# Half of a weight-gradient product placed one step earlier, and the first group's transposes in another order

## The chip, the cores and the metric

The kernel runs on one core of one Trainium2 chip. The metric is device time in microseconds (us), the median of several runs; lower is better. Five engines work side by side, each through its own list of instructions: TensorE (PE; its weight loads are PEld), VectorE (DVE), ScalarE (ACT), GpSimd (POOL) and SyncE (SP). The last two, and ScalarE near the end, also issue DMAs. The matrix products leave TensorE through PSUM, from where ScalarE or VectorE copies them out.

## The reference: what is computed

One layer's forward pass and its gradients, for x of 2048 x 576, a hidden width of 4608, and bf16 inputs:

```
g = sigmoid((x * gate_w).sum(-1))
a = irfft2(rfft2(x) * (w_r + 1j * w_i))                # spectral branch
b = (gelu(B_x @ w_gate) * (B_x @ w_up)) @ w_down       # FFN branch
out = g * a + (1 - g) * b
```

The outputs are out and the gradients for x, w_r, w_i, w_gate, w_up, w_down and gate_w. The function takes B_x as a constant, and the kernel reads one x. With dO the gradient of out, and A = gelu(x w_gate) * (x w_up), the FFN's part needs these products: z = dO w_down^T; xy = x [w_gate, w_up]; d_w_down = A^T dB, where dB is dO scaled by 1 - g; d_w_gate and d_w_up = x^T dH, where dH holds the two gradients of the hidden layer; and b and the gradient of x, which sum over the whole hidden width and come in a second phase.

## The kernel before

**Groups and steps.** The hidden width is cut into 18 groups of 256 columns, numbered from 0 (`for g in range(NG)`, L986). A group has four steps (`for m in range(NPR)`, L988); each takes 512 of the 2048 rows as four tiles of 128. In the prediction "third step" is m = 2 and "fourth step" is m = 3 (the sets x1, do1 and do2 of the first group are counted from 1, and its steps are called by m). One step does this:

- `H_mm` (L403) issues z: 16 matmuls of 256 columns (L413) and 4 of half height (L418), into a tile of the PSUM pool `pz`, and then the start of xy (L422). `full` adds 8 matmuls of 512 columns (L429) for each half of xy.
- ScalarE evicts z with the factor 1 - g (`H_da`, da, L441) and each half of xy (`H_act`: q L448, xb L450, hu L451). The tile q of the first half needs a buffer that VectorE's previous step must have left (L489).
- VectorE makes dH and A of it (`H_ew1` L456 to L460, then `H_ew2` L483 to L491, with sigmoids on ScalarE between, s and sg, L476 to L480). SP stores them in DRAM for the second phase (L495).

**Weight gradients one group late.** While group g goes through its steps, TensorE also forms the weight gradients of group g - 1. `W_units` (L514) lists them: w[0] to w[3] are the four row blocks of the d_w product (L553), 16 matmuls of 512 columns each, cut into four pieces of 4 matmuls; d[0] to d[3] are the parts of d_w_down (L535), 16 matmuls of 288 columns each; `tail` (L563) is the last 64 rows of d_w, put between z and xy of the third step. The returned list says which pieces go into which step: entries 0 to 3 are the steps, entry 4 is carried into the first step of the next group (`carry`), and the dictionary holds what is put inside a step. The results go into the pool `pw` (two PSUM banks, tag wps); ScalarE copies each out (L504) and POOL's queue stores it.

**Units of the spectral branch.** From the second group on, the list `fft` (L927) is worked off between the pieces: forward transforms (L596, L613), the middle (L705, L794), and the inverse (L841, L853, L867 with L869). Each unit is 2 to 8 short matmuls into a `pf` tile, and ScalarE copies it out (Y L601 or L603, ve L616, Xx and Xg L710, Vt L797, ZT L844, ZU L856, ev L873). `pf` and `z` are one tag in `pz`, which has a single buffer of two banks. So a unit can't start before the unit or z ahead of it has been copied out. `want` (L951) says how many units a step gets, and the loop at L1081 spreads them over the step's pieces by weight. In the middle part VectorE also forms the spectral products (`side`, L997): L722 to L764, run after `H_ew1` of each step.

**The first group** has no weight gradients to do yet. Its steps transpose x and dO on TensorE instead (`titems`, L370): a set of tiles is three items of 8, 8 and 4 transposes (L378, L384), each into a tile of the pool `pg`, which has two buffers, and a copy on ScalarE (AC) or VectorE (VC) after each (L385). The gate (`gate`, L389; its activation g_bf is L396) takes a `pg` tile too. In step m, x1 is the set of x for step m + 1, and do2 the set of dO for step m + 2. In the code, `early` runs before the first half of xy, `mid_` after it, and `rest` between z's full matmuls and its half-height ones in the next step.

**Order of the work.** Each engine runs its instructions in the order in which the code issues them; nothing moves them later. Semaphores between the engines come from the tile framework. DMAs also share eight semaphores in turn (one can wait for an earlier one that has the same semaphore).

**Second phase.** After the groups, SP loads `pin` tiles (L1126) and `wd_all` (L1145), while TensorE works off the last group's weight gradients (L1148 to L1153); their stores are issued by ScalarE. Then 1.2 thousand matmuls each over `wgT`, `wuT` and `wd_all` (L1201) form the gradient of x and b.

Of the kernel before, what the change touches and what calls it, by code (L numbers as in the profile page):

```python
# [255 lines left out]
def kernel(  # L256
# [246 lines left out]
    def wevac(out, in_):  # L503
        wcopy[0](out, in_)  # L504
# [3 lines left out]
    def dwtile(name):  # L508
        if not spare:
            return stage.tile([P, 2, FG], BF16, tag="dw", name=name)  # L510
        spare.append(spare.pop(0))
        return ew.tile([P, 4, FG], BF16, tag=spare[-1], name=name, bufs=2)[:, 0:2, :]

    def W_units(g):  # L514
        fsl = slice(g * FG, (g + 1) * FG)
        kt = kept[g]

        def tl(k, t):
            tile_ = kt[t // 4][min(k, 1)]
            return tile_[:, t % 4, :] if k == 0 else tile_[:, t % 4, k - 1, :]  # L520
        dwd_tiles, wp = {}, {}

        def halves(f, us):
            return [(us, lambda: f(0)), (us, lambda: f(1))]

        def wtile(key):
            if key not in wp:
                wp[key] = pw.tile([P, TPB, FG], F32, tag="wps", name="wps")
            return wp[key]

        def u_dwd(fch, h):
            def f(half):
                wps = wtile(("d", fch, h)).rearrange("p a b -> p (a b)")
                for t in range(8 * half, 8 * half + 8):
                    nc.tensor.matmul(wps[:, :288], lhsT=tl(0, t)[:, fch * P:(fch + 1) * P],  # L535
                                     rhs=dB[:, t, h * 288:(h + 1) * 288], start=(t == 0), stop=(t == T - 1))
                if half == 0:
                    return
                if h == 0:
                    dwd_tiles[fch] = stage.tile([P, D], BF16, tag="dwd", name="dwd")  # L540
                dwd = dwd_tiles[fch]
                wevac(dwd[:, h * 288:(h + 1) * 288], wps[:, :288])
                if h == 1:
                    r0 = g * FG + fch * P
                    wst[0].dma_start(out_6[r0:r0 + P, :], dwd[:])
            return halves(f, 1.0)

        def u_dw(c, cuts=(0, 4, 8, 12, T)):

            def f(t0, t1):  # L550
                wps = wtile(("w", c))
                for t in range(t0, t1):
                    nc.tensor.matmul(wps[:].rearrange("p a b -> p (a b)"), lhsT=xn[:, t, c * P:(c + 1) * P],  # L553
                                     rhs=kt[t // 4][1][:, t % 4].rearrange("p k f -> p (k f)"), start=(t == 0), stop=(t == T - 1))
                if t1 < T:
                    return
                dw = dwtile("dw")
                wevac(dw[:], wps[:])
                for k, ov in enumerate((o4v, o5v)):
                    wst[0].dma_start(ov[:, c, fsl], dw[:, k, :])  # L560
            return [(3.45 * (b - a) / T, lambda a=a, b=b: f(a, b)) for a, b in zip(cuts, cuts[1:])]

        def tail():  # L563
            wps = wtile("t")
            for t in range(T):
                for k, r in ((1, LO), (2, HI)):
                    nc.tensor.matmul(wps[r, 0, :], lhsT=xn[:, t, 512:576], rhs=tl(k, t),  # L567
                                     start=(t == 0), stop=(t == T - 1))
            dw = dwtile("dwt")
            wevac(dw[:, 0], wps[:, 0, :])  # L570
            wst[0].dma_start(out_4[512:576, fsl], dw[LO, 0, :])
            wst[0].dma_start(out_5[512:576, fsl], dw[HI, 0, :])
        w = [u_dw(c, (0, 12, T)) if g == 0 and c < 2 else u_dw(c) for c in range(4)]
        d = [u_dwd(fch, h) for fch in range(FCH) for h in range(2)]
        if g == 0:
            return [[w[0][:1], w[1][:1]], [w[2]], [d[0], d[1], d[2], d[3]], [w[3][:3]], w[3][3:], {1: [w[0][1][1], w[1][1][1]], 2: [tail]}]
        return [[d[0]], [d[1], d[2], d[3]], [w[0]], [w[1], w[2]], w[3], {2: [tail]}]


    side = []  # L580
# [311 lines left out]
    for c in range(6):  # L892
        w = gwr[0:1, eo(c)] if c < 4 else gwr[0:1, 512:D]
# [83 lines left out]
    carry, pend, held, rest = [], None, [], []  # L977
# [8 lines left out]
    for g in range(NG):  # L986
# [3 lines left out]
        for m in range(NPR):  # L990
# [15 lines left out]
            if g == 0:  # L1006
                def items(src, dst, t, *cp):
                    return titems(src, dst, 4 * t, (pgtile,) * 3, cp) if t < NPR else [None] * 3
                do1 = items(dB, dOT, 1, VC, VC, VC) if m == 0 else []
                do2 = items(dB, dOT, m + 2, AC, AC, VC)  # L1010
                x1 = items(xn, xT, m + 1, AC if m else VC, VC, VC)
                z, xy_full = H_mm(g, m, ([opening] if m == 0 else []) + rest)
                rest = []
                da = H_da(g, m, z)
                if m == 0:
                    early, mid_, late_ = do1[:2], [do1[2], x1[0]], x1[1:]
                elif m < NPR - 1:
                    early, mid_, late_ = x1[:1], x1[1:], []
                else:
                    early, mid_, late_ = [], [], []  # L1020
                for f in early:
                    f()
                xy = xy_full(0)
                for f in mid_:
                    f()
                if held:
                    held.pop()()
                for part in (1, 0):
                    H_act(0, xy, tiles, part)

                def between():
                    for f in late_:
                        f()
                xy = xy_full(1, between)
                for part in range(2):
                    H_act(1, xy, tiles, part)
                if m == 0:
                    build_R(nc, tb, unit, 4)
                    columns_B(nc, tb, res)
                elif m == 1:  # L1040
                    next(makeB)
                if m < NPR - 1:
                    gate(m + 1)
                else:
                    V.tensor_copy(g32[:], g_bf[:])
                    V.tensor_scalar(gs32[:], g32[:], SD2, None, op0=ALU.mult)
                if m + 2 < NPR:
                    do2[0]()
                    rest = do2[1:]
                state += [*H_ew1(g, tiles, da), da]  # L1050
                held.append(sigs)
            else:
                z, xy_full = H_mm(g, m)
                da = H_da(g, m, z)
                for f in inside:
                    f()
                xy = xy_full(0)
                if held:
                    scale_dB(0, AC)
                    held.pop()()  # L1060
                for part in (1, 0):
                    H_act(0, xy, tiles, part)
                k0 = int(n > 0 and pr > 7 and ready())
                xy = xy_full(1, fft_next if k0 else None)
                for part in range(2):
                    H_act(1, xy, tiles, part)
                state += [*H_ew1(g, tiles, da), da]
                if pr == 5:
                    scale_dB(1, AC)
                    scale_dB(2, VC)  # L1070
                    build_R(nc, tb, unit, 8)
                    build_R(nc, tb, unit, 12)
                elif pr == 6:
                    scale_dB(3, VC)
                    next(makeB)
                side_work(4.4)
                jobs = carry + hs
                total = sum(w for w, _ in jobs)
                at, k = 0.0, k0
                tables = {6: 0}.get(pr)  # L1080
                for i, (w, f) in enumerate(jobs):  # L1081
                    if k < n and (at >= total * k / n - 0.45 or len(jobs) - i <= n - k):
                        fft_next()
                        k += 1
                    if i == tables:
                        run_late(tb)
                        wcopy[0] = VC
                    if pr == NG * NPR - 1 and at == 0.0:
                        sigs()
                    f()  # L1090
                    at += w
                wcopy[0] = AC
                while k < n:
                    fft_next()
                    k += 1
                flush()
                if pr == 6:
                    next(makeB)
                if pr < NG * NPR - 1:
                    sigs()  # L1100
# [250 lines left out]
```

## Time and profile before

| | us |
|---|---|
| median of 3 runs (1407.67 to 1407.96) | 1407.94 |
| the profiled execution: device time | 1407.67 |
| its span, from the first to the last instruction | 1405.8 |
| TensorE busy | 1375.1 |
| VectorE busy | 748.8 |
| ScalarE busy | 712.3 |
| the first group, first z to the second group's first z | 8.3 to 45.3 |
| second phase's first matmul | 977.7 |

How to read the profile: times are us from the start of the span. A line of the timeline gives start, length, engine, line of the code, operation, what it writes and reads, its shape and how many follow each other; in square brackets, how long the engine stood idle before it and whose work ended that. A line of the waits gives the waiting instruction, an arrow, whose work it waited for, and then the sum in us, the count and the longest. Matmul ends are modelled: one takes longer than its distance to the next, so that what counts between two is start to start. A matmul of 512 columns takes 0.216 us so (sixteen in 3.45 us); a few records are missing, which the counts show (x11 for 12).

### The profile page before, as it was taken

Reading aid. Unit: us, or ns where it says so; the run is one execution under the profiler, and the core shown is the slowest. Engines: PE = TensorE matmul, PEld = TensorE weight load, DVE = VectorE, ACT = ScalarE, POOL = GpSimd, SP = SyncE. Lnnn points to the kernel's source line nnn. Section 1 sums busy time; section 2 is a strip of 40 time slices with the busy share of each in tenths; the row PEclk is TensorE's granted clock in tenths of the full one; section 3 lists DMA queues with packets and bytes.
Section 4 is the critical chain, followed back from the end, with each engine's and each line's share of the span. In section 5 each row is a group of like instructions: output and inputs, shape, how many; then the busy total and the mean of one; then the engine's idle time right before and its main releaser. Section 6 shows DMA issues by size and latency. Waiting matters only on the chain.

```text
span 1405.8 us, 25935 instructions
## 1 busy us (share of the span) xinstructions
PE 1375.1 (98%) x10182; PEld 913.9 (65%) x10272; DVE 748.8 (53%) x1408; ACT 712.3 (51%) x1309; POOL 246.0 (18%) x486
## 2 busy tenths in 40 slices
PE   8999999999999999999999999999999999999999
PEld 6556566565556556556566566556777777777777
DVE  7975656555888778885666666560000642212101
ACT  7867767777778777767777776661000000000000
POOL 3001111023353633423101111110000100000000
PEclk9999999999999999999999999999999999999999
DMA  6423434355464555556456464849999997778774
GB/s 217 127 81 109 130 109 129 91 143 157 111 160 134 152 156 156 127 145 164 129 140 174 127 167 132 197 116 281 182 193 186 239 190 169 160 160 166 156 152 90
DMA packets 510646, 214.49 MB, mean 153 GB/s; under 512 B 312538, under 2 KB 503708, under 8 KB 510524
## 3 DMA queue, kind: packets, MB, share of 16 engines
q1 hardware_dynamic: 493402, 187.44, 57.2%
q0 software_dynamic: 14912, 24.24, 6.2%
q8 instruction: 80, 1.31, 0.4%
q10 hardware_dynamic: 2210, 1.15, 0.3%
q14 instruction: 42, 0.34, 0.1%
HBM read 41.05 MB, written 93.84 MB: 96 GB/s over the span
## 4 chain that ended last, share of the span: by engine, by line
PE 55%; ACT 1%; DMA 1%; SPq 1%; DVE 1%; issue 1%; ACTq 0%
PE acc L1201 30%; PE wps L553 7%; PE xy L429 7%; PE wps L535 4%; PE z L413 4%; PE wps L567 1%; DMA wd_all<-in_B_w_down_dram 1%; PE xy L422 1%; SPq L1126 1%; PE z L418 1%; PE pf L867 1%; PE pf L869 1%; ACT ZT L844 0%; PE pf L841 0%; ACT hu L451 0%
## 5 line engine op out<-in xcount | busy, mean ns | idle before, releaser
L1201 PEld LDWEIGHTS <-pin 128*128 128x128 bf16 x3456 | 338.0, 98 | 86.2 <-issue 0.9
L553 PE MATMUL wps<-dH,xn 128*128 128x512 bf16 x1124 | 268.1, 379 | 1.5
L429 PE MATMUL xy<-wgu,xT 128*128 128x512 bf16 x1090 | 257.9, 379 | 8.5 <-issue 7.8
L429 PEld LDWEIGHTS <-xT 128*128 128x128 bf16 x1152 | 106.5, 98 | 133.0 <-issue 24.8
L553 PEld LDWEIGHTS <-xn 128*128 128x128 bf16 x1152 | 111.4, 98 | 118.4 <-issue 0.6
L1218 ACT COPY bo<-acc 128x288 f32<-128x288 f32 x32 | 12.7, 398 | 304.4 <-PE acc L1201 279.8
L535 PE MATMUL wps<-dB,A 128*128 128x288 bf16 x1152 | 154.2, 286 | 1.0 <-DVE dB L984 0.9
L560 POOL DMA_DIRECT2D out_dram<-dw x134 | 72.7, 546 | 443.3 <-ACT dw L504 417.8
L1201 PE MATMUL acc<-wgT,pin 128*128 128x288 bf16 x1152 | 143.9, 286 | 0.3 <-ACT dw L504 0.3
L1201 PE MATMUL acc<-wuT,pin 128*128 128x288 bf16 x1152 | 143.6, 286 | 0.0
L1201 PE MATMUL acc<-wd_all,pin 128*128 128x288 bf16 x1152 | 142.6, 286 | 0.0
L413 PE MATMUL z<-wdT,dOT 128*128 128x256 bf16 x1152 | 137.5, 272 | 3.6 <-ACT Xg L710 1.0
L535 PEld LDWEIGHTS <-A 128*128 128x128 bf16 x1152 | 112.1, 98 | 34.7 <-issue 1.9
L413 PEld LDWEIGHTS <-dOT 128*128 128x128 bf16 x1152 | 112.4, 98 | 26.6 <-issue 6.4
L441 ACT ACTIVATE da<-z,omg 128x256 bf16<-128x256 f32 x288 | 112.1, 472 | 16.0 <-PE z L418 15.9
L450 ACT CAST xb<-xy 128x512 bf16<-128x512 f32 x144 | 85.2, 592 | 48.2 <-PE xy L429 48.2
L1273 DVE SCALAR_TENSOR_TENSOR f32t<-gwf,dlog,b16t 128x576 f32<-128x576 f32 x16 | 13.1, 817 | 173.4 <-DMA b16t<-dxa_scr 173.4
L448 ACT ACTIVATE q<-xy 128x512 bf16<-128x512 f32 x144 | 87.7, 612 | 17.1 <-DVE xb L489 8.7
L483 DVE TENSOR_TENSOR xb<-xb,sg 128x1024 bf16<-128x1024 bf16 x48 | 33.2, 692 | 104.1 <-ACT sg L479 104.1
L451 ACT CAST hu<-xy 128x512 bf16<-128x512 f32 x144 | 87.6, 608 | 0.0
L504 ACT CAST dw<-wps 128x512 bf16<-128x512 f32 x72 | 42.2, 588 | 68.2 <-PE wps L553 57.4
L1232 DVE SCALAR_TENSOR_TENSOR b16t<-b16t,g,f32t 128x576 bf16<-128x576 bf16 x16 | 13.1, 819 | 96.1 <-DMA b16t<-a_scr 95.8
(216 smaller groups left out, 1655.3 us busy)
## 6 DMA issues: line engine op xcount, KB each, us to landing
scr<-dH SPq DMA_DIRECT2D x144, 256.0 KB, 3.4
scr<-A SPq DMA_DIRECT2D x72, 256.0 KB, 2.7
out_dram<-dw POOLq DMA_DIRECT2D x134, 64.0 KB, 2.5
wd_all<-in_B_w_down_dram SPq DMA_DIRECT2D x3, 1728.0 KB, 12.2
out_dram<-dwd POOLq DMA_DIRECT2D x34, 144.0 KB, 2.9
scr_p<-Vt SPq DMA_DIRECT2D x32, 145.0 KB, 2.8
wgu<-in_B_w_gate_dram SPq DMA_DIRECT2D x18, 256.0 KB, 4.1
wgu<-in_B_w_up_dram SPq DMA_DIRECT2D x18, 256.0 KB, 3.4
```

What stands on the lines that cost most here:

```text
L413: nc.tensor.matmul(zo(t), lhsT=dOT[:, ci, t, :], rhs=wdT[:, ci, :], start=(t % 4 < 2 and ci == 0), stop=False)
L429: nc.tensor.matmul(xy[k][:, t % 2, :], lhsT=xT[:, ci, t, :], rhs=wgu[:, ci, :], start=False, stop=(ci == 3))
L441: nc.scalar.activation(da[:, t, :], z[:, t % 2, t // 2, :], ACT.Copy, scale=omg32[:, 4 * m + t:4 * m + t + 1])
L448: nc.scalar.activation(q[:, h, :], xy[:, :, 0:FG], ACT.Square)
L450: nc.scalar.copy(xb[:, h, :], xy[:, :, 0:FG])
L451: nc.scalar.copy(hu[:, h, :], xy[:, :, FG:2 * FG])
L483: V.tensor_tensor(xb[:], xb[:], s[:], op=ALU.mult)
L504: wcopy[0](out, in_)
L535: nc.tensor.matmul(wps[:, :288], lhsT=tl(0, t)[:, fch * P:(fch + 1) * P], rhs=dB[:, t, h * 288:(h + 1) * 288], start=(t == 0), stop=(t == ...
L553: nc.tensor.matmul(wps[:].rearrange("p a b -> p (a b)"), lhsT=xn[:, t, c * P:(c + 1) * P], rhs=kt[t // 4][1][:, t % 4].rearrange("p k f -> ...
L560: wst[0].dma_start(ov[:, c, fsl], dw[:, k, :])
L1201: nc.tensor.matmul(acc[:, :288], lhsT=src[:, r, :], rhs=w_of(r)[:, h * 288:(h + 1) * 288], start=(first and r == 0), stop=(last and r == F ...
```

## The change

In the lists of the groups from the second on, the first two of w[1]'s four pieces (8 of its 16 matmuls of 512 columns) stand in the third step's entry, behind w[0], instead of the fourth's. In the first group's steps 1 and 2, two of the three items of x1 run before the first half of xy instead of one; and in steps 0 and 1, two of the three items of do2 run at the end of the step instead of one, so that a single one is left for the next step's z.

```
@@ W_units @@
         if g == 0:
             return [[w[0][:1], w[1][:1]], [w[2]], [d[0], d[1], d[2], d[3]], [w[3][:3]], w[3][3:], {1: [w[0][1][1], w[1][1][1]], 2: [tail]}]
-        return [[d[0]], [d[1], d[2], d[3]], [w[0]], [w[1], w[2]], w[3], {2: [tail]}]
+        return [[d[0]], [d[1], d[2], d[3]], [w[0], w[1][:2]], [w[1][2:], w[2]], w[3], {2: [tail]}]
@@ first group @@
                 if m == 0:
                     early, mid_, late_ = do1[:2], [do1[2], x1[0]], x1[1:]
                 elif m < NPR - 1:
-                    early, mid_, late_ = x1[:1], x1[1:], []
+                    early, mid_, late_ = x1[:2], x1[2:], []
@@ first group @@
                 if m + 2 < NPR:
                     do2[0]()
-                    rest = do2[1:]
+                    do2[1]()
+                    rest = [do2[2]]
```

More of the change, by code (lines that the diff above doesn't have):

```diff
@@ L576, in W_units @@
             return [[w[0][:1], w[1][:1]], [w[2]], [d[0], d[1], d[2], d[3]], [w[3][:3]], w[3][3:], {1: [w[0][1][1], w[1][1][1]], 2: [tail]}]
-        return [[d[0]], [d[1], d[2], d[3]], [w[0]], [w[1], w[2]], w[3], {2: [tail]}]
+        return [[d[0]], [d[1], d[2], d[3]], [w[0], w[1][:2]], [w[1][2:], w[2]], w[3], {2: [tail]}]
     side = []
@@ L1017 @@
                 elif m < NPR - 1:
-                    early, mid_, late_ = x1[:1], x1[1:], []
+                    early, mid_, late_ = x1[:2], x1[2:], []
                 else:
@@ L1048 @@
                     do2[0]()
-                    rest = do2[1:]
+                    do2[1]()
+                    rest = [do2[2]]
                 state += [*H_ew1(g, tiles, da), da]
```

## The prediction

> **What bounds the kernel now.** The page comes first. TensorE is busy for 98% of the span, its clock row shows 9 in all forty slices, and the chain that ended last is 55% TensorE. Only time in which TensorE waits can be won; no matmul is added or removed.
>
> ```profile
> span 1405.8 us, 25935 instructions
> ...
> PE 1375.1 (98%) x10182; PEld 913.9 (65%) x10272; DVE 748.8 (53%) x1408; ACT 712.3 (51%) x1309; POOL 246.0 (18%) x486
> ...
> PEclk9999999999999999999999999999999999999999
> ```
>
> Second, the waits of TensorE from 99 to 853 us, the stretch in which the spectral branch's units lie between the FFN's matmuls.
>
> ```profile
> PE pf L596 <- ACT ve L616: 1.8, 4, 1.1
> PE pf L705 <- ACT Xx L710: 1.8, 4, 0.8
> PE pf L867 <- ACT ZT L844: 1.4, 2, 1.1
> PE pf L705 <- ACT Xg L710: 1.2, 2, 0.6
> PE z L413 <- ACT Xg L710: 1.0, 2, 0.5
> ```
>
> All of them are one wait: a unit (pf) or the next z needs the single PSUM buffer of the pool pz, and ScalarE hasn't yet copied the unit before out of it. Third, where they lie. I cut the timeline at each step's first z matmul, and took each unit's start less the start of the instruction before it and its own length. So counted, the third steps (m = 2) of groups 2 to 15 hold 11.67 us: 0.45, 0.70, 1.09, 1.83, 1.75, 0.84, 0.68, 1.75, 0, 0, 0, 1.51, 0.40, 0.67. The fourth steps hold 2.13 us: 1.13 in group 8, 0.93 in group 10, 0.08 in group 14. (The waits list shows some 0.17 us less for each, since it starts at the modelled end.) Without units a third step lasts 11.38 us (878.44 to 889.83) and a fourth 12.97 (to 902.80): the third has the least to put between units. Here is that of group 9:
>
> ```profile
> 514.63 0.41 PE L705 MATMUL pf<-Vp,Btab 128*128 128x289 bf16 x2
> 514.88 1.89 PE L553 MATMUL wps<-dH,xn 128*128 128x512 bf16 x8
> 517.39 0.41 PE L705 MATMUL pf<-Vp,Btab 128*128 128x289 bf16 x2 [0.62 <-ACT Xg L710]
> 517.63 1.03 PE L553 MATMUL wps<-dH,xn 128*128 128x512 bf16 x4
> 519.17 1.91 PE L413 MATMUL z<-wdT,dOT 128*128 128x256 bf16 x16 [0.51 <-ACT Xg L710]
> ```
>
> After the last unit (517.39) the two copies of L710 start at 517.83, 0.20 us after the next matmul, and take 1.28; z follows 0.05 later. That is 1.53 us, and four matmuls of L553 cover 0.86 (sixteen take 3.45 in the chain): 0.67 us is lost. The unit before is late because ScalarE must first evict the second half of xy (q, xb, hu).
>
> **The third step gets eight matmuls.** In the changed program's order w[1][:2] lies behind w[0] in 16 third steps (groups 2 to 17), and the gaps between units grow: 4, 4, 4 to 8, 4, 8 where four units lie in a step, 4, 8, 4 to 8, 8, 8 where three do. In the fourth step 8, 8, 8 becomes 4, 8, 4 or 8, and 12, 8, 12 becomes 8, 8, 8. No engine's order of work changes else, but that the eviction of w[0] or w[1] falls between other copies; two batches of loads on POOL's queue (Wt, needed a pair of units later) come behind two dw stores; SP's queue keeps its order.
>
> In group 9 the second unit moves from 514.63 to 515.21 (four matmuls, 0.86, less its own wait of 0.29); the third is due at 517.18, ScalarE is free for it at 517.39 as before: 0.21 left. z has 1.73 to cover 1.53. So 1.75 becomes 0.21, and the fourth step (slacks of 2.07, 0.70 and 1.57 us before its units and the next z) keeps none: 1.54 won. The same sum for each group:
>
> Groups 2 to 5. What waits behind q, xb and hu gets 0.86 us more cover; a unit with gap 4 and an idle ScalarE loses only 0.03 to 0.14. Third steps: 0.45, 0.70, 1.09, 1.83 become 0.03, 0.14, 0.41, 1.35 (group 5 keeps its table transposes); fourth steps get 0.03, 0.03, 0.14, 0. **Won 1.9.**
>
> Groups 6 to 11. Here VectorE takes part: q has one buffer, so the step's first q eviction waits until VectorE has finished the step before.
>
> ```profile
> ACT q L448 <- DVE xb L489: 8.4, 5, 2.6
> ```
>
> This is from ScalarE's waits between 330 and 640 us. It strikes fourth steps: q starts there 6.4, 6.7, 7.3, 7.9 and 8.2 us after z in groups 6, 7, 8, 10, 11, against 5.5 in others. VectorE runs through there without a gap, so its times stand while the fourth step now starts later: q comes 0.2 to 1.7 us earlier in the step, at 6.2, 5.8, 6.1, 6.2, 6.5. Third steps: 1.75, 0.84, 0.68, 1.75, 0, 0 become 0.20, 0, 0.12, 0.21, 0, 0; fourth: group 8 1.13 to about 1.4 (the dw copy now precedes the unit's copy), group 10 0.93 to 0.66. But a shorter fourth step leaves VectorE late in the next group. After group 6 its first copy (L483) waits for nothing in three steps on end, so the unit at 398.94 can't come earlier: all 1.55 is lost again. After group 7 (0.84) some 0.5 stays, after group 10 nothing, while group 9's is kept (VectorE idles 1.55 us in the next step). Passed on: 0, 0.5, 0.25, 1.54, 0, 0. **Won 2.3.**
>
> Groups 12 to 17. Third steps 13 to 15: 1.51, 0.40, 0.67 to 0.84, 0, 0.04 (ZT takes 1.02 us, and stays late once in group 13). Group 14's fourth step has five units and now gaps of 4, 4, 8, 4, 4: the wait of 0.35 that its third step shows, and 0.4 before z, move there: 0.08 to 0.8. Groups 12 and 15 get 0.05 each; 16 and 17 have no units. **Won 0.9.** Together 5.1 us.
>
> **Behind the last step.** ScalarE's last dw copy stands behind a DMA issue that waits for the second wd_all load (978.54), so TensorE stands 0.43 us at 979.55. The load starts with the last step, which now has 1.73 us less behind it, and would hold TensorE as much longer; but in the changed program that issue shares its semaphore with other transfers, and the wd_all one falls to the very last dw store, which nobody needs. I take 0.4 won; bounds: 0.43 won, 1.7 lost.
>
> **The first group.** The second set of dO transposes leaves the z of steps 1 and 2 and stands at the end of the step before; the second set of x transposes goes ahead of xy_full(0). The copies keep their order on ScalarE and VectorE; only TensorE meets them sooner. pg has two buffers, so each set needs the copy of the set two before.
>
> ```profile
> 29.45 0.64 PE L394 MATMUL pf<-gwT,xT 128*128 128x1 bf16 x20
> 29.95 0.61 PE L378 MATMUL pf<-ident,dB 128*128 128x128 bf16 x8
> 30.39 1.91 PE L413 MATMUL z<-wdT,dOT 128*128 128x256 bf16 x16
> ...
> 36.35 0.61 PE L378 MATMUL pf<-ident,xn 128*128 128x128 bf16 x8 [0.17 <-DVE dOT L385]
> ```
>
> The set now at 32.14 must wait for the gate's buffer, which g_bf (ScalarE, 31.08 to 31.29) frees; z stood in that hole. At the first border: transposes end at 21.42, g_bf at 22.21, z starts at 22.69, not 21.42; the step ends 0.48 late. At the second: transposes end at 30.9, g_bf at 31.8, z starts at 32.25 in place of 30.39. Then x's second set, now ahead of eight xy matmuls, meets VectorE's dOT copy, which stands behind L460 and ends at 36.37: it starts at 36.42, and so do, behind it, the eight matmuls that had run from 34.51. Step 3's z comes at 41.07, 1.83 late. In the second group TensorE already waits 0.78 us at 48.37 for hu, whose chain through VectorE's L483 is 1.37 late; so **1.4 lost**. Bounds: nothing lost (ScalarE has almost no gap from 21 to 38.6 us and may set the end alone); 2.8 (the three waits, 0.83, 0.90 and 1.07, in full).
>
> A rule against this part: TensorE: Matmul & The Clock Gate, section "A second HAM failure mode: psum-queue depth-cycling", says that short idle spells between matmul groups can make the clock fall back and warm up again. The trace shows no such fall: the stretch 5 to 45 us, with idle spells up to 0.96 us, has a granted clock of 1.00. By the rule, with half clock for its window of some 3.4 us, two such spells would cost 3.4 us more and leave about 1407; that is an estimate from the page, and I don't take it.
>
> **Sum.** 5.1 + 0.4 - 1.4 = 4.1 us. The profiled execution took 1407.67 us (span 1405.8 and 1.9 around it), 0.27 under the median of 1407.94. 1407.67 - 4.1 = **1403.6 us**.
>
> **Rivals.** *The waits change places.* A fourth step without units is now 11.24 us, as short as the third was (11.38); if it collects the third's waits, nothing is won but the 0.4, and the first group costs 1.4: 1408.7. For it: group 14. Against: the moved cover leaves both steps with 24 matmuls, and first steps with gaps of 8, 4, 12 lose 0.03 to 0.4.
>
> *All is kept.* VectorE gives back what groups 6, 7 and 10 lost (1.55, 0.34, 0.27) and the first group costs nothing: 1407.67 - 7.3 - 0.4 = 1400.0. Against it: L483 without a wait in those steps.
>
> *Slower: VectorE moves with the step.* If its copies of the fourth step start only with the later end of the third, q doesn't come earlier. The second unit of a fourth step is now due 8.03 us after z (5.20 + 0.24 + 0.86 + 1.73) and needs q's start + 0.6 + 1.28 + 0.05; beyond q at 6.1 every matmul taken away is a wait. In groups 6, 7, 8, 10, 11 that is up to 5 x 1.73 = 8.6; the eight other groups with units mirror the third step's 7.0. Saved: 11.67 less group 5's 1.35, 10.3. Net 5.3 + 1.4 - 0.4: 1414. Against it: L483 starts there without a gap, held by VectorE's own queue and not by ScalarE.
>
> **Chances.** Forecast (1401.5 to 1405.5) 0.50, places changed 0.25, all kept 0.12, slower 0.13. The range 1400.0 to 1409.0 takes in the first three and most bounds of the first group; the slower case is left out. A measurement of this kernel can tell about 0.2% (2.8 us) from no change. Faster by more: 0.57 (forecast but its upper end, and all kept); within: 0.30; slower: 0.13.
>
> **What would show it.** Third-step waits of groups 2 to 15 from 11.7 to about 3.3 us, fourth-step waits from 2.1 to about 3.2, with group 14's fourth step at 0.8. q in the fourth steps of groups 6 to 11 at 5.5 to 6.5 us; if it stays at 7 to 8, the slower rival holds. The wait at 398.94 grows in group 7's second step. Step 3's z at 41.1 (39.24 now), the second group's late xy matmul at 49.7 (48.37). The last dw copy right behind its matmul. Wrong would be the forecast if the first group lost over 3 us, or if fourth steps show over 6 us of waits.

## The result, and the profile after

The changed kernel takes 1403.21 us (median of 6 runs, 1403.08 to 1404.81); the kernel before, run beside it, 1407.81 us (6 runs, 1407.29 to 1409.18). The ratio is 0.9968, with a 95% interval from 0.9955 to 0.9981: 4.6 us, or 0.33%, faster. The profiled execution took 1403.11 us.

Its page, the lines that answer to the first fence of the prediction:

```profile
span 1401.2 us, 25933 instructions
...
PE 1373.5 (98%) x10187; PEld 913.6 (65%) x10272; DVE 748.9 (53%) x1408; ACT 710.7 (51%) x1309; POOL 245.1 (17%) x486
...
PEclk9999999999999999999999999999999999999999
```

The span is 4.6 us shorter; the clock row is the same, so none of this comes from the clock. The waits of TensorE from 99 to 853 us (the largest for which ScalarE is named):

```profile
PE pf L705 <- ACT Xx L710: 1.2, 2, 0.8
PE pf L705 <- ACT Xg L710: 1.1, 1, 1.1
PE pf L596 <- ACT ve L616: 1.1, 1, 1.1
PE pf L794 <- ACT Vt L797: 0.8, 2, 0.6
```

The list has the same shape as before, but shorter, and L794, which had not been at its head, has come in. Cut at each step's first z and counted as in the prediction, the third steps of groups 2 to 15 hold 3.06 us of waits (11.67 before), the fourth steps 3.0 (2.13 before). The first and second steps have got worse in groups 7, 8 and 11: group 7's from 0 and 0.54 to 0.95 and 1.15, group 8's second from 0.56 to 0.69, group 11's first from 0.21 to 0.57.

Group 9's third step, which the prediction showed with two waits in brackets, now has none long enough for a bracket:

```profile
513.56 0.41 PE L705 MATMUL pf<-Vp,Btab 128*128 128x289 bf16 x2
513.81 1.89 PE L553 MATMUL wps<-dH,xn 128*128 128x512 bf16 x8
515.74 0.41 PE L705 MATMUL pf<-Vp,Btab 128*128 128x289 bf16 x2
515.99 1.89 PE L553 MATMUL wps<-dH,xn 128*128 128x512 bf16 x8
517.71 1.91 PE L413 MATMUL z<-wdT,dOT 128*128 128x256 bf16 x16
```

Eight matmuls of 512 columns (x8) now stand behind the last unit where four stood, and z no longer waits: ScalarE copies the unit out while they run. Counted from start to start, 0.21 us is left before the last unit (515.74), where 0.79 stood.

Where the time went can be read off one table: how much earlier (minus) or later a z starts than in the kernel before, with the start of group 0's first z set equal (in these executions it lies up to 0.33 us to either side of the kernel before, also where the work ahead of it is the same).

| first z of | after | new list, first group as before | first group as after, old list |
|---|---|---|---|
| step 1 of group 0 | +1.29 | 0 | +1.29 |
| step 2 of group 0 | +2.06 | 0 | +2.06 |
| step 3 of group 0 | +2.02 | 0 | +2.02 |
| group 2 | +1.66 | 0 | +1.66 |
| group 6 | -0.37 | -2.02 | +1.66 |
| group 7 | -1.90 | -3.54 | |
| group 7, third step | -0.37 | -2.02 | |
| group 9 | -1.44 | -3.10 | |
| group 10 | -2.97 | -4.63 | |
| group 12 | -2.95 | -4.58 | |
| group 17 | -3.94 | -5.56 | +1.62 |

So the list won 5.6 us by group 17, the first group cost 1.65, and behind the last step another 0.43 was won (3.94 + 0.43 + 0.2 of the start is the 4.6 of the span). Group 6 wins 1.53 us in its third step and has given all of it back by group 7's third step.

### The profile page after: what moved, and what is told of

It reads as the page before. It is cut to its first block, busy times and chain, and to the rows that moved or that the text cites. A ratio compares the mean times of both kernels' runs of the same rounds, so it can differ in the third digit from the quotient of the medians.

```text
span 1401.2 us, 25933 instructions
## 1 busy us (share of the span) xinstructions
PE 1373.5 (98%) x10187; PEld 913.6 (65%) x10272; DVE 748.9 (53%) x1408; ACT 710.7 (51%) x1309; POOL 245.1 (17%) x486
## 3 DMA queue, kind: packets, MB, share of 16 engines
q10 hardware_dynamic: 2210, 1.15, 0.3%
HBM read 41.05 MB, written 93.84 MB: 96 GB/s over the span
## 4 chain that ended last, share of the span: by engine, by line
PE 56%; DVE 1%; ACT 1%; issue 0%; DMA 0%; SPq 0%; DVEq 0%; ACTq 0%
PE acc L1202 30%; PE wps L553 7%; PE xy L429 6%; PE wps L535 4%; PE z L413 3%; PE wps L567 1%; PE xy L422 1%; PE z L418 1%; PE pf L867 1%; PE pf L869 1%; ACT ZT L844 0%; PE pf L841 0%; ACT q L448 0%; DMA wdT<-wdT 0%; ACT Xg L710 0%
## 5 line engine op out<-in xcount | busy, mean ns | idle before, releaser
L483 DVE TENSOR_TENSOR xb<-xb,sg 128x1024 bf16<-128x1024 bf16 x48 | 33.2, 691 | 95.5 <-ACT sg L479 95.4
L456 DVE TENSOR_SCALAR s<-q 128x1024 bf16<-128x1024 bf16 x72 | 30.7, 426 | 67.1 <-ACT q L448 67.1
```

The source lines that it names most:

```text
L483: V.tensor_tensor(xb[:], xb[:], s[:], op=ALU.mult)
```

## The experiments

Theory: the time is that of three parts which add up. Eight matmuls are cover for a unit's copy, and are worth more between the third step's units than between the fourth's; what a group wins can be taken back by VectorE, which ScalarE meets at q; and the first group's transposes, moved forward, wait for copies that come no earlier. Rivals: the list is worth nothing but for its end; the two parts hide each other; any cover in the third step is good, and the more the better.

**The two parts alone.** First the list alone, with the first group as before the change:

```
-        return [[d[0]], [d[1], d[2], d[3]], [w[0]], [w[1], w[2]], w[3], {2: [tail]}]
+        return [[d[0]], [d[1], d[2], d[3]], [w[0], w[1][:2]], [w[1][2:], w[2]], w[3], {2: [tail]}]
```

> The kernel before with the new list alone (eight matmuls of w[1] in the third step), the first group as before. Theory (the list won some 5.6 us up to the last group and 0.4 behind it, the first group's order cost 1.4 to 1.6): step 3's z at 39.2 us again, no wait at 36.4 other than the 0.17 of before, and 1401.7 us, that is 1.5 below the changed kernel. Rival (the first group's order costs nothing in the end, ScalarE sets it): 1403.2, as the changed kernel. Rival (the first group's new order was a gain as well): over 1404.

Measured: 1401.47 us (1401.38 to 1402.02, 5 runs), ratio 0.9954 (0.9941 to 0.9968). It is faster than both kernels. Then the first group alone, the other half of the diff:

```
-                    early, mid_, late_ = x1[:1], x1[1:], []
+                    early, mid_, late_ = x1[:2], x1[2:], []
...
                     do2[0]()
-                    rest = do2[1:]
+                    do2[1]()
+                    rest = [do2[2]]
```

> The kernel before with the first group's new order alone, the old list. Theory: the first group's z of step 3 comes 1.8 us late, the second group starts 1.4 late and nothing takes that back: 1409.3 us. The third-step waits stay at 11.7 us, and so does TensorE's 0.43 us behind the last dw copy, since the wd_all load keeps its semaphore. Rival (something later takes the delay up): 1407.8. Rival (a gain): under 1407.

Measured: 1409.15 us (11 runs), ratio 1.0010 (1.0001 to 1.0018). The medians give -6.2 and +1.4, together -4.8; the change gave -4.6. The parts add up, and the table above shows that neither changes the other's steps.

**The halves of the first group's part**, each beside the new list: only the do2 edit, and only the x1 edit of the diff above.

> The new list, and of the first group's change only the two items of dO at the end of the step (x as before). Theory: waits of some 0.8 and 0.9 us for g_bf at 22.2 and 31.8, none for VectorE's dOT copy above 0.2; step 3's z some 0.8 late (40.0), the second group's steps some 0.75 late, 0.75 us over the kernel with the list alone. Rival (each half of the first group's change has its own share, and they add up to 1.4): with the next kernel the two sum to 1.4 us.

> The new list, and of the first group's change only the two items of x before the first half of xy (dO as before). Theory: no wait for g_bf, but in step 2 the second item of x meets VectorE's dOT copy with nothing in front of it: a wait of about 1.9 us that ends near 36.4; step 3's z about 1.7 late (40.95), the second group about 1.3 late: 1.3 us over the kernel with the list alone. With the dO half (0.75) that is more than both together (1.4), because both wait for much the same chain on ScalarE and VectorE. Rival (they add up): 0.65 or less.

Measured: 1402.56 and 1403.27 us (one run each). By the z of group 2, with equal starts, do2 alone costs 1.11 us, x1 alone 1.15, both 1.66: the halves don't add, and the do2 half costs more than expected by itself. Where they meet is seen in the timelines of step 2. With do2 alone the second set of x transposes still stands behind seven matmuls of xy:

```profile
35.12 0.62 PE L378 MATMUL pf<-ident,xn 128*128 128x128 bf16 x8
...
37.30 0.61 PE L378 MATMUL pf<-ident,xn 128*128 128x128 bf16 x8
```

With x1 alone it stands ahead of them:

```profile
36.46 0.61 PE L378 MATMUL pf<-ident,xn 128*128 128x128 bf16 x8 [1.51 <-DVE dOT L385]
```

And in the changed kernel, with both:

```profile
31.80 0.61 PE L378 MATMUL pf<-ident,dB 128*128 128x128 bf16 x8 [0.78 <-ACT g_bf L396]
...
36.43 0.61 PE L378 MATMUL pf<-ident,xn 128*128 128x128 bf16 x8 [0.75 <-DVE dOT L385]
...
49.80 0.39 PE L422 MATMUL xy<-wgu,xT 64*128 64x512 bf16 x2 [0.24 <-ACT hu L451]
```

VectorE's copy of dOT lets the set go 27.86 us after step 0's first z with x1 alone (36.46 less 8.60) and 28.37 after it with both (36.43 less 8.06): only 0.51 apart, although step 2 begins 0.16 us late in the one and 2.06 in the other. With do2 alone the set comes behind the copy and loses nothing there, and the step makes up 0.94 of its 2.06. With x1 alone TensorE stands for 1.51; with both it comes later to the same copy and stands for 0.75. Largely it is the later of two times, not their sum. Step 3's z was expected 0.8 late with do2 alone and came 1.12 late, and the late xy matmul of the second group took up none of it (its wait is 0.61, as before the change).

**One group alone.** The new list in the steps of group 6 only:

```
+        if g == 5:
+            return [[d[0]], [d[1], d[2], d[3]], [w[0], w[1][:2]], [w[1][2:], w[2]], w[3], {2: [tail]}]
         return [[d[0]], [d[1], d[2], d[3]], [w[0]], [w[1], w[2]], w[3], {2: [tail]}]
```

> Only the third and fourth steps of one group, group 6, get the new list; all else is as before the change. Theory (the 1.55 us that group 6's third step wins are given back at once, since VectorE's L483 runs without a gap there and group 7's units wait for copies that wait for it): the third step's waits go from 1.75 to about 0.2 us, group 7's first z comes 1.5 us earlier, the waits of group 7's first and second step grow by 1.5 together, and group 8's first z comes within 0.3 us of where it was; the whole takes 1407.8 as before. Rival (the gain of each group is kept): group 8's first z comes 1.5 us earlier, and the whole takes 1406.3.

Measured: 1407.45 us (one run), where the kernel before took 1407.52. With equal starts group 7's first z comes 1.51 us earlier, its second step's 0.58 earlier, its third step's 0.04 later, group 8's 0.03 later. Two units of group 7's first two steps, in the kernel before:

```profile
383.74 0.41 PE L794 MATMUL pf<-qn,BTtab 128*128 128x290 bf16 x2
...
398.94 0.41 PE L705 MATMUL pf<-Vp,Btab 128*128 128x289 bf16 x2 [0.38 <-ACT Xx L710]
```

And in this one (its lines from 577 on are numbered two higher, so L794 is L796 and L705 is L707):

```profile
383.04 0.41 PE L796 MATMUL pf<-qn,BTtab 128*128 128x290 bf16 x2 [0.60 <-ACT Vt L799]
...
399.03 0.41 PE L707 MATMUL pf<-Vp,Btab 128*128 128x289 bf16 x2 [0.83 <-ACT Xx L712]
```

The gain of 1.5 us is there at the border and is gone two steps later, mostly in these two waits for ScalarE, with no other group changed. That a group's gain was given back is thus shown, not only argued.

**All sixteen.** The whole of w[1] in the third step:

```
-        return [[d[0]], [d[1], d[2], d[3]], [w[0]], [w[1], w[2]], w[3], {2: [tail]}]
+        return [[d[0]], [d[1], d[2], d[3]], [w[0], w[1]], [w[2]], w[3], {2: [tail]}]
```

> All 16 matmuls of w[1] in the third step and only w[2] in the fourth, first group as before the change. Theory (matmuls between units are cover, and eight are the balance between two steps): third-step waits fall from 3.1 to about 1.5 us, since little is left there, while the fourth step, now 9.5 us long without units and so shorter than the third step of before (11.38), holds 8 to 12 us of waits where eight moved matmuls left it 3.0. VectorE's q, which comes another 1.7 us earlier in the fourth step at best, gives some of that. The whole: 1401.5 + 5 to 9 = 1406.5 to 1410.5. Rival (it only matters that the third step gets cover, since the fourth waits for VectorE and not for its own units): fourth-step waits of 3 to 4 us and 1400 to 1401.5 for the whole.

Measured: 1415.86 us (1414.10 to 1419.65, 4 runs), ratio 1.0068 (1.0053 to 1.0084): slower than before, and by more than expected. Third steps hold 1.35 us of waits, fourth steps 13.2, and first and second steps of groups 7, 8, 10 and 11 have 4.4 us more than with eight moved. Of the 13.2, 5.8 lie in group 8's fourth step, and there the cause is another one, which ScalarE's waits from 330 to 640 us show:

```profile
ACT q L448 <- DVE s L489: 9.6, 7, 3.1
ACT dw L504 <- DMA out_dram<-dwt: 5.1, 1, 5.1
```

The second line is one copy of a dw that stood 5.1 us, for the store of the tail's dwt from the same two stage tiles: w[0] and w[1] now both end in the step that the tail stands in. Without that group the fourth steps hold 7.4, just under what was expected. The first line is the q wait of the steps after (1.6 us before the change, 4.1 after it). So eight is the best of the three: with 0, 8 and 16 matmuls moved the times are 1407.8, 1401.5 and 1415.9. Of the 14.4 us between eight and sixteen some 4.4 are group 8's fourth step (5.8 against 1.4 of waits); by this estimate sixteen would still be slower than none without them.

**Two buffers for q.** If what takes back group 6's gain is VectorE by way of q's only buffer, a second buffer should keep the gain. It needs 2 KB in each partition. The first attempt took them from the half-table pool and from the stage of dwd; the same without the second q is its control.

```
-    ... tc.tile_pool(name="half", bufs=3, side="right") ...
+    ... tc.tile_pool(name="half", bufs=2, side="right") ...
-                    dwd_tiles[fch] = stage.tile([P, D], BF16, tag="dwd", name="dwd")
+                    dwd_tiles[fch] = stage.tile([P, D], BF16, tag="dwd", name="dwd", bufs=1)
```

> The new list alone, with one buffer less in each of two pools that the next kernel needs the room of (two halves of a table in place of three, one dwd stage tile in place of two). A control: if neither buffer holds anything back, the time is that of the new list alone, 1401.5 within 0.7; if the dwd stage does, the first steps' copies of dwd wait for its store and the time is over 1402.5.

```
-            return ... ew.tile([P, 4, FG], BF16, tag=tag, name=tag, bufs=1)
+            return ... ew.tile([P, 4, FG], BF16, tag=tag, name=tag, bufs=2 if tag == "q" else 1)
```

> As the control, and two buffers for q in place of one, so that ScalarE's first q eviction of a step needn't wait until VectorE has finished with the q of the step before. Theory (what group 6's gain was given back to is VectorE, by way of q's buffer): q in the fourth steps of groups 6 to 11 starts at 5.5 us after z in place of 5.5 to 6.5, in group 7's first step at 5.5 in place of 7.45, the waits of group 7's first and second step (0.95 and 1.15) and of group 8's second and fourth (0.69, 1.37) mostly go, and the whole takes 1401.5 - 2.5 = 1399.0. Rival (VectorE is late in its own right: the next thing that ScalarE needs from it, xb of the step before at L489 or the z evictions' room, holds the same copies by as much): the waits stay with another releaser and the time is that of the control, 1401.5.

Measured: control 1409.19 us (one run), with two buffers for q 1403.17 (1401.27 to 1404.37, 5 runs). The room was not free. ScalarE's waits of the control, 330 to 480 us:

```profile
ACT dwd L504 <- DMA out_dram<-dwd: 5.1, 2, 3.8
```

A copy of dwd stands up to 3.8 us for the store before it, and what is behind it on ScalarE stands too. The absolute forecast missed (1399.0), but the two kernels differ by 6.0 us (4.8 to 7.9 over the five runs, against the one of the control). In the kernel with two q buffers group 7's first step has no wait of a unit (0.95 after), and its second step's last unit waits 0.05 (1.00). So I gave dwd and dw one stage of three tiles together, which is smaller than two of each; and in the kernel with the new list group 14's steps, which had lost by it, got the old one (`g == 13`: the list of group 13's gradients). The edits of half and of q above stay:

```
-            return stage.tile([P, 2, FG], BF16, tag="dw", name=name)
+            return stage.tile([P, D], BF16, tag="dw", name=name, bufs=3)[:, 0:2 * FG].rearrange("p (a b) -> p a b", a=2)
-                    dwd_tiles[fch] = stage.tile([P, D], BF16, tag="dwd", name="dwd")
+                    dwd_tiles[fch] = stage.tile([P, D], BF16, tag="dw", name="dwd", bufs=3)
...
+        if g == 13:
+            return [[d[0]], [d[1], d[2], d[3]], [w[0]], [w[1], w[2]], w[3], {2: [tail]}]
```

> The new list (but for the steps of group 14, which keep the old one), the first group as before the change, two buffers for q, and the room for the second one taken so that no store holds ScalarE: dwd and dw share one stage of three tiles in place of two each, and the half-table pool has two tiles. Theory: the 5 us by which ScalarE waited for dwd's single stage tile in the kernel before this one go, the waits of groups 7, 8, 10 and 11 stay as small as two buffers for q made them there (together 4.1 us under those of the new list alone), and group 14 gives back 0.3: 1401.5 - 4.4 = 1397.1. Rival (three shared tiles hold the copies up too, or ScalarE meets VectorE elsewhere): over 1400.

> The old list with the two buffers for q and the shared stage. Theory (the list is worth more when VectorE no longer takes back what a group wins): the waits of the second and fourth steps of groups 7, 8 and 10 shrink by some 2.5 us, the third steps keep their 11.7, the whole takes 1405, and the difference to the new list is about 8 us in place of 6.1. Rival (two buffers for q are worth the same under either list): 1403.3, a difference of 6.1.

Measured: new list 1396.73 us (1396.71 to 1398.41, 5 runs), ratio 0.9924 (0.9910 to 0.9937), the fastest kernel of this study (1397.1 was expected); old list 1404.11 (one run). With equal starts the list is worth 7.2 us by group 17 in this pair (0.3 of it by leaving group 14 out) and 5.6 without the second buffer. By the times the pair differs by 7.4, of which 0.3 is group 14; the 7.1 left lies halfway between the theory's 8 and the rival's 6.1. So the second buffer doesn't only keep what the list wins: under the old list it takes 3.6 us off (1407.72 to 1404.11), 3.0 of it by group 17's first z, where the waits in the second and fourth steps of groups 7, 8 and 10 are gone. Group 6's gain is kept whole: 1.54 us at group 7's first z, and still 1.54 at its third step's. The remaining waits of TensorE from 99 to 853 us, all but those put down to "issue" and three of 0.6 us or less (lines two higher again, L598 for L596):

```profile
PE pf L598 <- ACT ve L618: 1.1, 1, 1.1
PE z L413 <- ACT ve L618: 0.8, 1, 0.8
PE pf L707 <- ACT Xg L712: 0.5, 1, 0.5
```

L794's and Xx's lines are gone. From 330 to 640 us no q waits for VectorE any more: q starts 5.50 us after z in every first, second and fourth step of groups 6 to 11.

**Less work for VectorE.** The same question from the other side, with the old and the new list:

```
-                (0.8, mul("o1", G, X[:, :, 0, :])), (0.8, mul("o2", G, X[:, :, 1, :])), (0.85, comb("o1", "o2", True)),
...
-                o = st[p, "o1"]
+                o = st[p, "g"]
```

> As before the change, but VectorE leaves out the products o1 and o2 and their combination in the spectral branch, and the tile g is stored in their place, so d_w_r and d_w_i are not computed. Some 2.4 us of VectorE's work go per pair of units. Theory: VectorE is late less often in groups 7 to 11, q's buffer comes free earlier, and the whole takes 1405.5 to 1407; third-step waits stay near 11 us.

> The new list alone with the same products left out. Theory (VectorE's load decides how much of group 6's, 7's and 10's gain is kept): group 6's 1.55 us are no longer given back in group 7, and the difference to the old list with the same products left out is about 8 us; 1397.5 to 1399.5. Rival (what takes group 6's gain back is not VectorE's load): a difference of 6.1 as with all products, group 7's waits as they were.

Measured: 1405.78 and 1400.46 us (one run each). By group 17 the list is worth 5.7 us here, as with all products (5.6), and by the times 5.3: the expected 8 is refuted, and the rival's 6.1 is nearer. Group 7's first step still loses 1.0 us, since ScalarE still waits there for q:

```profile
379.96 0.60 ACT L448 ACTIVATE q<-xy 128x512 bf16<-128x512 f32 x1 [1.91 <-DVE s L489]
```

VectorE's timelines say why. The last spectral product ahead of that step's L483 is this one with the new list and all products:

```profile
375.64 0.76 DVE L730 TENSOR_TENSOR o<-Xg,Xx 128x1156 bf16<-128x1156 bf16 x1
```

and this one with the products left out:

```profile
375.84 0.76 DVE L730 TENSOR_TENSOR m<-Xx,Wt 128x1156 bf16<-128x1156 bf16 x1
```

The next pair's product has moved up into the room, so L483 and L489 come no earlier in this step (L489 6.7 us after z in the one, 6.8 in the other). The first effect is in group 7's second step, where the old list's wait (0.54) goes and the new list's shrinks from 1.00 to 0.55; group 8's fourth step follows (1.13 to 0.43 under the old list). So the edit does not lighten VectorE where most of group 6's gain is taken back, and the run says nothing against q's buffer as the place. It shows that VectorE's total load is not the measure: what counts is how late L489 is in that one step.

## Why the prediction was right

The sum had 5.1 us for the list, 0.4 behind the last step and 1.4 lost in the first group, 4.1 in all; measured are 5.6, 0.43 and 1.65, 4.4 in all, and 0.2 in the start of the first z. The two larger misses, 0.5 too little won and 0.25 too little lost, partly cancel. The fourth steps' 3.0 us refute the rival in which the waits change places.

**The move of eight matmuls** was put at 5.1 us and won 5.6. By stretches, in the changed kernel: groups 2 to 5 2.0 (1.9), groups 6 to 11 2.6 (2.3), groups 12 to 17 1.0 (0.9). The third-step waits came out as 0.03, 0.14, 0.30, 1.35, then 0.21, 0, 0.05, 0.21, 0, 0, and 0.73, 0, 0.04 in groups 13 to 15, against 0.03, 0.14, 0.41, 1.35, then 0.20, 0, 0.12, 0.21, 0, 0, and 0.84, 0, 0.04. The fourth steps of groups 8, 10 and 14 hold 1.37, 0.57 and 0.80 (1.4, 0.66, 0.8).

**VectorE's part** was right for group 6 in its amount, and was tested most directly by the one-group run. There the unit at 398.94 in fact comes no earlier (399.03, from a first z 0.05 later). But the prediction named only this unit's wait, in group 7's second step; 0.94 of the 1.53 us goes already in the first step, where q starts 7.45 us after z (5.91 before), and 0.59 in the second. q in the fourth steps of groups 6, 7, 8, 10 and 11 starts at 6.19, 5.83, 6.19, 6.15 and 6.49 (6.2, 5.8, 6.1, 6.2, 6.5), so the slower rival, in which VectorE moves with the step, is refuted. Of group 7's gain 0.69 was kept (0.5), of group 8's 0.38 (0.25), of group 9's 1.53 (1.54), of group 10's nothing. In group 9 the two units start at 513.56 and 515.74, which is 515.21 and 517.39, as worked out, less the 1.65 us by which that step starts earlier. ScalarE's q waits show where it went, from 330 to 640 us:

```profile
ACT q L448 <- DVE s L489: 4.1, 4, 1.8
ACT q L448 <- DVE xb L489: 2.8, 5, 0.9
```

The second line was 8.4 us before and stands in fourth steps; the first was 1.6 and stands in the first and second steps of the next groups. What the prediction put too simply is "the unit can't come earlier" because L483 runs without a gap: with two buffers for q, L483 still runs without one in these steps, and the unit comes 1.1 us earlier in its step (10.52 us after z in place of 11.61). The limit is the buffer through which ScalarE meets VectorE, not VectorE's queue itself. The loss came out right although this step of the reasoning doesn't hold by itself.

**The first group** was put at 1.4 and cost 1.65, with its three waits as worked out: 0.68, 0.78 and 0.75 by the profile's brackets, step 3's z at 41.05 (41.07), the late xy matmul at 49.80 (49.7). Before the change that matmul was

```profile
48.37 0.39 PE L422 MATMUL xy<-wgu,xT 64*128 64x512 bf16 x2 [0.61 <-ACT hu L451]
```

Its wait fell from 0.61 to 0.24, so 0.37 of the lateness went into a wait that was there already. The rival in which all is kept fails on this and on group 6.

**Behind the last step** 0.43 was won (0.4). ScalarE's last dw copy, in the kernel before:

```profile
978.92 0.58 ACT L504 CAST dw<-wps 128x512 bf16<-128x512 f32 x1 [3.92 <-DMA wd_all<-in_B_w_down_dram]
```

In the changed kernel it waits for nothing but its matmul:

```profile
973.71 0.59 ACT L504 CAST dw<-wps 128x512 bf16<-128x512 f32 x1 [2.87 <-PE wps L553]
```

The wait for the second wd_all load is gone. The semaphore numbers in the two traces agree with the reason given: before, that load and the store issued at 978.54, ahead of the last copy, both have number 100; in the changed kernel the load has 102, and so has the store issued at 976.86, 2.6 us after the last copy, with no copy behind it. The other end, 1.7 lost under the old order of semaphores, was not tried.

**The clock.** From 5 to 45 us the granted clock is 1.00 in the changed kernel, with three new idle spells of 0.68 to 0.78 us between groups of matmuls (and one of 0.97, as before the change), and 1.00 in the x1 run, with one of 1.51. The rule of the Trainium skill that was weighed (TensorE: Matmul & The Clock Gate, "A second HAM failure mode: psum-queue depth-cycling") did not show itself here; the estimate from it would have left about 1407.

## What to carry to other kernels

Matmuls between two users of one buffer are cover, so move them from steps with slack to steps without, and stop where the giving step runs out: half the piece won 6 us, the whole one lost 8, part of it by a stage tile. Before counting a gain, ask whether the next steps start on another engine's late queue: a step that ends earlier there can just wait longer, and the cure here was a second buffer where the engines meet, with room taken from a place that a run has shown to hold nothing up. Where two edits make the same engine wait for the same copy, the cost is nearer the later of the two times than their sum, so halves of an edit that wait for the same copy must not be added.

## What was not expected

- One stage tile instead of two for a store of 144 KB cost 7.7 us in the control (1401.47 to 1409.19, one run), which had a smaller half-table pool as well, but no wait of ScalarE is put down to that. Copies stood up to 3.8 us on ScalarE from 330 to 480 us; the store that held the longest of them landed 4.1 us after its issue (2.7 is the median from 392 to 404 us), and everything that ScalarE still had to evict stood behind it.
- Three stage tiles shared by two users do nearly as well as two for each: ScalarE waited once for them (0.8 us, for a dw store) and once for the smaller half-table pool (1.0 us), and TensorE's list shows no new wait. They are smaller, and the room was worth 4.7 us as a second buffer for q (1401.47 to 1396.73, 0.3 of it from group 14) under the new list, and 3.6 under the old one. That the shared stage itself costs nothing was not tried apart from the second buffer.
